# Where a layer-norm tile is transposed: by DMA or on TensorE, in the last forward pair of a four-layer attention kernel

## The chip, the cores and the metric

The kernel runs on one core of a Trainium2 chip, as one launch. The metric is the device time of that launch in microseconds. Before the change the median of seven runs is 2477.54 us (2466.08 to 2485.54).

## What is computed

Four residual layers run over a sequence of 2048 rows of width 640, with 32 heads of 20 columns. Layers 0 and 2 are of kind A (linear attention), layers 1 and 3 of kind B (softmax attention in a causal window of 256 rows). Both A layers share their weights, as do both B layers. The kernel returns the output and the gradients of the input and of the four weights.

```python
x = A_x
x = x + _A_ref(_layernorm(x), A_wqkv, A_wo)
x = x + _B_ref(_layernorm(x), B_wqkv, B_wo)
x = x + _A_ref(_layernorm(x), A_wqkv, A_wo)
x = x + _B_ref(_layernorm(x), B_wqkv, B_wo)
# _A_ref: phi(q) @ (sum over rows of phi(k)^T v), divided by phi(q) . sum phi(k); then @ wo
# _B_ref: softmax(q k^T * 20**-0.5 inside the window) @ v; then @ wo
# returned: x, and the vjp of x for grad_out with respect to A_x and the weights
```

## The kernel before

The rows lie in 16 tiles of 128. The forward pass has a first segment (the first half of layer 0) and two calls of `seg_pair`: the first finishes layer 0, runs layer 1 and begins layer 2; the second, which the text calls the last pair, finishes layer 2, runs layer 3 and already begins the backward pass (it computes dO, the gradient at the attention's output). The backward pass follows, in stages of its own, and reads what the forward pass stored.

`seg_pair` interleaves two streams. One is the attention itself: for each tile b and each of 8 groups g of four heads it makes scores (L410), exponentials on ScalarE (L416), masks on GpSimd (L419, L422) and products with the values (L438). The other is `step(b)`, a Python generator that walks through a list called `plan`: pairs of a function and an offset, so that `(qkv, 1)` in step b works on tile b + 1. Each function yields how many matmul columns it has issued; the loop takes pieces from the generator until the amount `work`, spread over the 8 groups, is reached. In the last pair the functions are: `mix`, the read-out of layer 2 and its transposed tile oT; `proj1`, the output projection of layer 2 and the layer norm before layer 3; `qkv`, the q, k and v of layer 3; `fetch_g`, which loads and transposes grad_out; `proj2`, the output projection of layer 3; and `do`, which computes dO. The first three steps (b = -3 to -1) run ahead of the attention; after that `steady[0]` is true.

The layer norm is `ln`. It makes statistics on VectorE (L217, L219), the reciprocal deviation on ScalarE (L221, L223) and the normalised rows ln_hn on VectorE (L225). The matmuls of qkv (L358) need these rows transposed, as ln_hnT. In steady tiles `pt()` is None, and a DMA on SyncE's queue does that (`tr`, L152). Otherwise `flip` does it: five TensorE transposes against the identity (L715) into a PSUM tile and one copy out (L717). SyncE also stores the plain rows for the backward pass (L125, hn).

`B_qkv` ends with three DMA transposes of its q, k and v slabs into the ring tiles (L152), from which the scores read, and with stores of the ring to DRAM (`keep`, the tensor qkvT) on ScalarE's DMA queue, half a pair of tiles in each call.

A tile scheduler turns this traced order into one order for each engine, by readiness and priority, and hands out the tiles of a pool as they come free. Four PSUM banks (pool `psd`, the tiles named d) serve all projections, transposes and value products; two tiles (`pss`, the tiles named s) hold scores. Each engine then works through its own order strictly, and each DMA queue too.

Of the kernel before, what the change touches and what calls it, by code (L numbers as in the profile page):

```python
# [16 lines left out]
P = 128  # L17
# [6 lines left out]
class Kern:  # L24

    def __init__(self, ctx, tc, x0, A_wqkv, A_wo, B_wqkv, B_wo, grad_out, outs):
# [4 lines left out]
        self.H = H = D // DH  # L31
        self.G = H // 4
        self.TT = TT = T // P
# [74 lines left out]
        for l in (1, 3):  # L108
            self.sv[l] = dict(
                qk=d.tile([P, TT, 2 * D], BF, name=f"qk{l}"),  # L110
                qkvT=d.tile([P, 3 * self.G, T], BF, name=f"qkvT{l}"),
                dOT=d.tile([P, self.G, T], BF, name=f"dOT{l}"),
                dO=d.tile([P, TT, D], BF, name=f"dO{l}"))
# [95 lines left out]

    def ln(self, l, tt, pw, pt=None):
        nc, D = self.nc, self.D
        x = self.car[:, tt, :]
        st = pw.tile([P, 2, nc.vector.BN_STATS_DIM], F32, name="ln_st")
        for c in range(2):
            nc.vector.bn_stats(st[:, c, :], x[:, c * self.HD:(c + 1) * self.HD])  # L217
        mv = pw.tile([P, nc.vector.BN_AGGR_DIM], F32, name="ln_mv")
        nc.vector.bn_aggr(mv, st)  # L219
        lv = pw.tile([P, 1], F32, name="ln_lv")  # L220
        nc.scalar.activation(lv, mv[:, 1:2], ACT.Ln, bias=self.eps_t, scale=1.0)  # L221
        rs = self.rs[l][:, tt:tt + 1]
        nc.scalar.activation(rs, lv, ACT.Exp, scale=-0.5)  # L223
        hn = pw.tile([P, D], BF, name="ln_hn")
        nc.vector.tensor_scalar(out=hn, in0=x, scalar1=mv[:, 0:1], scalar2=rs, op0=ALU.subtract, op1=ALU.mult)  # L225
        hnT = pw.tile([P, self.DT, P], BF, name="ln_hnT")
        if pt is None:
            self.tr(hnT, hn)
        else:
            self.flip(hn, self.DT, hnT, pt, [nc.scalar.copy])  # L230
        self.dma(self.hn_d[l][:, tt, :], hn, nc.sync)
        return hnT

    def flip_o(self, l, tt, o, pw, pt=None):
        oT = pw.tile([P, self.DT, P], BF, name="oT")
# [113 lines left out]

    def B_qkv(self, l, tt, hnT, W, qk, v, ring, pps):  # L350

        nc = self.nc
        qkv = qk.rearrange("p (h d) -> p h d", d=HP)
        vv = v.rearrange("p (h d) -> p h d", d=HP)
        for ci in range(4):
            ps = pps.tile([P, 512], F32, name="d")[:, 0:480]
            for k in range(self.DT):
                nc.tensor.matmul(ps, lhsT=hnT[:, k, :], rhs=W[:, k, ci * 480:(ci + 1) * 480],  # L358
                                 start=(k == 0), stop=(k == self.DT - 1))
            h0, h1 = ci * 24, (ci + 1) * 24  # L360
            for t, base, n in ((qkv, 0, 2 * self.H), (vv, 2 * self.H, self.H)):
                a, b = max(h0, base), min(h1, base + n)
                if a < b:
                    dst, src = t[:, a - base:b - base, 0:DH], self.hv(ps)[:, a - h0:b - h0]
                    if ci % 2 == 0:
                        nc.vector.tensor_copy(dst, src)
                    else:
                        nc.scalar.copy(dst, src)  # L368
            yield self.DT * 480
        G = self.G  # L370
        for i, src in enumerate((qk[:, 0:G * P], qk[:, G * P:], v)):
            self.tr(self.ring_at(ring, i, tt), src)
        for i in range(2):
            flat = self.pw_fwd.tile([P, self.D], BF, name="qk_flat")
            nc.vector.tensor_copy(self.hv(flat), qkv[:, i * self.H:(i + 1) * self.H, 0:DH])
            self.store(self.sv[l]["qk"][:, tt, i * self.D:(i + 1) * self.D], flat)

        def keep(pair, i, g0, g1):
            src = self.ring_at(ring, i, 2 * pair, 2)
            return (self.sv[l]["qkvT"][:, i * G + g0:i * G + g1, 2 * pair * P:(2 * pair + 2) * P], src[:, g0:g1, :])  # L380
        parts = (((0, 0, G), (1, 0, G // 2)), ((1, G // 2, G), (2, 0, G)))
        if tt >= 2:
            for x in parts[tt % 2]:
                self.dma(*keep(tt // 2 - 1, *x))
        if tt == self.TT - 1:
            self.ring_tail = [keep(tt // 2, *x) for x in parts[0] + parts[1]]

# [99 lines left out]
    def seg_pair(self, l, acc, on_tail=None):  # L487

        nc, TT, H, G = self.nc, self.TT, self.H, self.G
        with ExitStack() as st:  # L490
            pW = self.pool(st, "fw")
            pw = self.pool(st, "fww", 2)
# [5 lines left out]
            last = l + 2 > 3  # L498
            if last:
                self.B_do_setup(pW, 2, 2)  # L500
            oT1, hn1, oT2, hn2 = {}, {}, {}, {}
            self.close_A(acc)
            mbd = self.mbd
            if not last:
# [12 lines left out]
            ring = [pW.tile([P, G, n * P], BF, name=f"ring{i}") for i, n in enumerate((4, 6, 4))]  # L517
            self.score_blocks, spreads = [], []
            tiles = []
            steady = [False]  # L520
# [10 lines left out]
            bank = Bank()  # L531

            def pt():
                return None if steady[0] else banks
# [6 lines left out]

            def proj1(t):
                yield from self.out_proj(t, oT1.pop(t), WoA, pps)
                hn1[t] = self.ln(l + 1, t, pw, pt())

            def qkv(t):
                yield from self.B_qkv(l + 1, t, hn1.pop(t), WB, qks[t % 2], slabs[t % len(slabs)], ring, pps)
# [30 lines left out]


            if last:  # L580
                plan = ((mix, 3), (qkv, 1), (proj1, 2), (fetch_g, -1), (proj2, -1), (do, -1))
                work, skip = 21300, (9600, 4600)
            else:
                plan = ((mix, 3), (qkv, 1), (proj1, 2), (first_half, -2), (proj2, -1))
                work, skip = 27000, (5000, 0)
# [931 lines left out]
```

## Time and profile before

| what | value |
|---|---|
| median of 7 runs | 2477.54 us (2466.08 to 2485.54) |
| the profiled execution's own time | 2485.54 us |
| its span, first to last instruction | 2483.8 us |
| granted TensorE clock, mean | 0.925 |
| busy: TensorE, VectorE, ScalarE, GpSimd | 88%, 62%, 49%, 40% |
| in 560:860 us, the steady tiles of the last pair | 84%, 71%, 59%, 58% |
| granted TensorE clock in 560:860 us | 0.94 |

A wait in the profile reads "who waited, for whom: total us, how often, the longest". A line of the timeline reads "start us, length us, engine, line, operation, written tile<-read tiles, shape, how many in a row [idle time before, and what ended it]". A line of windows gives the stretch and its length, then the busy time (and the number of instructions) of TensorE, its weight loads, VectorE, ScalarE and GpSimd, then the granted clock, the busy share of the DMA engines and GB/s.

### The profile page before, as it was taken

How to read it: one execution, taken by the hardware profiler on the slowest of the kernel's cores; microseconds unless marked ns; L12 is line 12 of the kernel's file. 1: busy time of each engine (PE TensorE's matmuls, PEld its weight loads, DVE VectorE, ACT ScalarE, POOL GpSimd, SP SyncE). 2: the span in 40 equal slices, each digit the busy share in tenths (PEclk: the TensorE clock that was granted, in tenths of full speed). 3: DMA queues.
4: the chain of work that ended last, by engine and by line, in shares of the span. 5: the costliest groups of instructions: out<-in, count | busy, mean ns of one | idle time of the engine just before them, and what ended most of it. 6: DMA issues, size and time to landing. Idle time of an engine off the chain costs nothing.

```text
span 2483.8 us, 68598 instructions
## 1 busy us (share of the span) xinstructions
PE 2179.1 (88%) x27602; PEld 1501.3 (60%) x27602; DVE 1544.2 (62%) x3022; ACT 1224.6 (49%) x1957; POOL 986.0 (40%) x1528
## 2 busy tenths in 40 slices
PE   6879989878788879999989799689999979979999
PEld 4635555544445536777657577467777756656455
DVE  6657767557766747778756577456676656646212
ACT  4447767635555646777733344455665543333000
POOL 4436656545555624444433333233343333311000
PEclk9989999978989957999989999689999979989999
DMA  8599888477888798797989596899988979588787
GB/s 248 149 186 202 185 176 179 130 175 171 199 181 183 178 260 160 151 158 139 189 187 235 131 242 192 217 219 197 189 178 168 192 175 232 151 228 231 191 268 217
DMA packets 895233, 474.37 MB, mean 191 GB/s; under 512 B 626752, under 2 KB 873280, under 8 KB 894912
## 3 DMA queue, kind: packets, MB, share of 16 engines
q1 hardware_dynamic: 782288, 338.72, 65.1%
q0 software_dynamic: 24768, 84.57, 10.4%
q10 hardware_dynamic: 87856, 46.68, 6.8%
q8 instruction: 216, 3.54, 0.6%
q14 instruction: 105, 0.86, 0.1%
HBM read 187.07 MB, written 161.19 MB: 140 GB/s over the span
## 4 chain that ended last, share of the span: by engine, by line
PE 36%; DMA 7%; issue 6%; DVE 5%; SPq 3%; POOL 2%; ACT 2%; ACTq 0%; DVEq 0%; POOLq 0%
PE acc L950 8%; PE acc L1024 7%; PE wg L1363 6%; PE sp L890 5%; PE d L758 5%; PE tp L934 3%; POOL do_o L738 2%; SPq L125 2%; PE t L715 1%; DVE ds L924 1%; ACT e L904 1%; DVE car L775 1%; DMA dsT<-ds 1%; DMA wg_r<-dqkv 1%; SPq L152 1%
## 5 line engine op out<-in xcount | busy, mean ns | idle before, releaser
L924 DVE SCALAR_TENSOR_TENSOR ds<-sp,e 128x768 bf16<-128x768 f32 (+2 forms) x512 | 462.9, 906 | 255.9 <-PE sp L890 159.6
L904 ACT ACTIVATE e<-sp 128x768 bf16<-128x768 f32 (+2 forms) x512 | 394.4, 777 | 238.4 <-PE sp L890 170.2
L416 ACT ACTIVATE e<-s 128x1024 bf16<-128x1024 f32 x360 | 359.9, 1025 | 139.8 <-PE s L410 113.6
L908 POOL TENSOR_SCALAR_AFFINE_SELECT e<-e 128x512 bf16<-128x512 bf16 x256 | 163.0, 637 | 422.9 <-ACT e L904 414.9
L410 PE MATMUL s<-qbd,ring 128*128 128x512 bf16 x720 | 247.9, 393 | 16.1 <-ACT e L416 12.2
L358 PE MATMUL d<-W,ln_hnT 128*128 128x480 bf16 x640 | 173.0, 405 | 42.2 <-DMA ln_hnT<-ln_hn 36.0
L1024 PEld LDWEIGHTS <-wg_l 128*128 128x128 bf16 x2800 | 191.4, 101 | 30.4 <-issue 13.3
L890 PE MATMUL sp<-VT,dOT 32*128 32x384 bf16 (+2 forms) x1024 | 181.3, 341 | 27.0 <-ACT e L904 23.1
L419 POOL TENSOR_SCALAR_AFFINE_SELECT e<-e 128x512 bf16<-128x512 bf16 x256 | 165.1, 646 | 96.2 <-ACT e L416 94.5
L890 PE MATMUL sp<-KT,QT 32*128 32x384 bf16 (+2 forms) x1024 | 185.3, 346 | 13.1 <-ACT e L904 6.0
L1363 PE MATMUL wg<-wg_r,wg_l 128*128 128x480 bf16 (+1 forms) x960 | 177.4, 348 | 5.3 <-DMA wg_r<-dqkv 2.8
L265 PE MATMUL d<-W,ln_hnT 128*128 128x320 bf16 x960 | 155.8, 312 | 29.4 <-ACT v_slab L368 11.9
L422 POOL TENSOR_SCALAR_AFFINE_SELECT e<-e 128x512 bf16<-128x512 bf16 x224 | 146.0, 652 | 85.9 <-ACT e L416 84.5
L1024 PE MATMUL acc<-wg_r,wg_l 128*128 128x160 bf16 x1840 | 157.6, 240 | 12.7 <-DMA wg_r<-dqkv 6.2
L758 PE MATMUL d<-WT,dqkvT 128*128 128x320 bf16 x960 | 145.5, 306 | 10.7 <-DMA dqkvT<-dqkv 10.7
L1363 PEld LDWEIGHTS <-wg_l 128*128 128x128 bf16 x960 | 95.0, 99 | 87.5 <-issue 7.9
L265 PEld LDWEIGHTS <-ln_hnT 128*128 128x128 bf16 x960 | 96.0, 101 | 83.1 <-issue 27.6
L438 PEld LDWEIGHTS <-e 128*128 128x128 bf16 x2880 | 113.0, 97 | 53.9 <-POOL e L419 9.7
L912 POOL TENSOR_SCALAR_AFFINE_SELECT e<-e 128x512 bf16<-128x512 bf16 x224 | 142.3, 635 | 0.0
L934 PE MATMUL tp<-ident,ds 128*128 128x128 bf16 x1440 | 136.0, 234 | 6.0 <-DVE ds L924 2.7
L358 PEld LDWEIGHTS <-ln_hnT 128*128 128x128 bf16 x640 | 65.8, 106 | 118.7 <-DMA ln_hnT<-ln_hn 43.7
L950 PEld LDWEIGHTS <-dsT 128*128 128x128 bf16 x2880 | 93.9, 98 | 68.2 <-issue 47.9
(192 smaller groups left out, 4395.7 us busy)
## 6 DMA issues: line engine op xcount, KB each, us to landing
qkvT<-ring ACTq DMA_DIRECT2D x32, 512.0 KB, 4.3
dqkv<-dqkv_o POOLq DMA_DIRECT2D x64, 240.0 KB, 4.1
wg_r<-dqkv SPq DMA_DIRECT2D x64, 240.0 KB, 4.4
hn<-ln_hn SPq DMA_DIRECT2D x64, 160.0 KB, 2.4
qk<-qk_flat POOLq DMA_DIRECT2D x64, 160.0 KB, 4.2
qk_r<-qk SPq DMA_DIRECT2D x32, 320.0 KB, 4.3
hn_ld<-hn SPq DMA_DIRECT2D x64, 160.0 KB, 3.2
dqkv<-dkv_t POOLq DMA_DIRECT2D x32, 320.0 KB, 4.4
```

Of the source, the lines that this page charges most:

```text
L265: nc.tensor.matmul(ps, lhsT=hnT[:, k, :], rhs=W[:, k, ci * HD:(ci + 1) * HD], start=(k == 0), stop=(k == self.DT - 1))
L358: nc.tensor.matmul(ps, lhsT=hnT[:, k, :], rhs=W[:, k, ci * 480:(ci + 1) * 480], start=(k == 0), stop=(k == self.DT - 1))
L410: nc.tensor.matmul(ps[:, i, :], lhsT=self.ring_at(ring, 1, kt)[:, g, :], rhs=self.qbd[b % 2][:, g, :, :], start=True, stop=True)
L416: nc.scalar.activation(e[:, 0:i + 1], ps[:, 0:i + 1], ACT.Exp, scale=self.c_att)
L758: self.nc.tensor.matmul(ps[:, c, 0:self.HD], lhsT=w, rhs=WT[:, k, c * self.HD:(c + 1) * self.HD], start=(k == 0), stop=(k == len(lhs) - 1))
L890: nc.tensor.matmul(ps[:, j, 0:nkt * P], lhsT=slabs[g][ta][r0:r0 + HP, b * P:(b + 1) * P], rhs=slabs[g][tb][r0:r0 + HP, k0 * P:(k0 + nkt) * P],
L904: nc.scalar.activation(ev[:, 2 * half:2 * half + 2], ps[:, :, 0:nkt * P].rearrange("p h (i k) -> p h i k", k=P), ACT.Exp, scale=c_att)
L924: nc.vector.scalar_tensor_tensor(out=dv[:, hs], in0=ps[:, :, 0:nkt * P].rearrange("p h (i k) -> p h i k", k=P), scalar=c_att, in1=ev[:, hs ...
L934: nc.tensor.transpose(tp[:, i * P:(i + 1) * P], ds_of[u][:, (nb + i) * P:(nb + i + 1) * P], self.ident)
L950: x.append(nc.tensor.matmul(acc[:, hh * DH:hh * DH + w], lhsT=lhsT, rhs=rhs(rname, g, t, hh, w), start=(i == 0), stop=(i == len(s) - 1), s ...
L1024: x = self.nc.tensor.matmul(ps[:, 0:w], lhsT=lhs(t), rhs=rhs(t), start=(t == 0), stop=(t == self.TT - 1), skip_group_check=True)
L1363: nc.tensor.matmul(ps, lhsT=lhs[:, tt, rows], rhs=rhs[:, tt, 0:w], start=(tt == 0), stop=(tt == TT - 1))
```

## The change

Three things change. `ln` can leave out the transposition (`later`) and return the rows and the empty tile; in steady tiles of the last pair a new function `flip_hn` then transposes them on TensorE, between `proj2` and `do` of the same step. The plan of the last pair is put in another order, with qkv and proj1 ahead of mix, and with slightly larger amounts in `work` and `skip`. In `B_qkv`, for both pairs, the stores of the ring are traced at the head of the function, before the matmuls and the new transposes. Line numbers after the diff are 2 to 13 higher.

```diff
@@ ln
-    def ln(self, l, tt, pw, pt=None):
+    def ln(self, l, tt, pw, pt=None, later=False):
...
-        if pt is None:
+        if later:
+            pass
+        elif pt is None:
             self.tr(hnT, hn)
         else:
             self.flip(hn, self.DT, hnT, pt, [nc.scalar.copy])
         self.dma(self.hn_d[l][:, tt, :], hn, nc.sync)
-        return hnT
+        return (hn, hnT) if later else hnT
@@ B_qkv
+        def keep(pair, i, g0, g1):
...
+        parts = (((0, 0, G), (1, 0, G // 2)), ((1, G // 2, G), (2, 0, G)))
+        if tt >= 2:
+            for x in parts[tt % 2]:
+                self.dma(*keep(tt // 2 - 1, *x))
         qkv = qk.rearrange("p (h d) -> p h d", d=HP)
...
-        def keep(pair, i, g0, g1):
...
-        if tt >= 2:
-            for x in parts[tt % 2]:
-                self.dma(*keep(tt // 2 - 1, *x))
@@ seg_pair
             def proj1(t):
                 yield from self.out_proj(t, oT1.pop(t), WoA, pps)
-                hn1[t] = self.ln(l + 1, t, pw, pt())
+                late = last and steady[0]
+                hn1[t] = self.ln(l + 1, t, pw, pt(), late)
+                if late:
+                    unflipped.append(t)
+
+            def flip_hn(t):
+                for x in unflipped:
+                    hn, hnT = hn1[x]
+                    self.flip(hn, self.DT, hnT, bank, [nc.scalar.copy])
+                    hn1[x] = hnT
+                unflipped.clear()
+                yield 640
...
             if last:
-                plan = ((mix, 3), (qkv, 1), (proj1, 2), (fetch_g, -1), (proj2, -1), (do, -1))
-                work, skip = 21300, (9600, 4600)
+                plan = ((qkv, 1), (proj1, 2), (mix, 3), (fetch_g, -1), (proj2, -1), (flip_hn, 2), (do, -1))
+                work, skip = 21900, (9600, 5200)
```

More of the change, by code (lines that the diff above doesn't have):

```diff
@@ L350, in B_qkv @@
     def B_qkv(self, l, tt, hnT, W, qk, v, ring, pps):
-        nc = self.nc
+        nc, G = self.nc, self.G
+        def keep(pair, i, g0, g1):
+            src = self.ring_at(ring, i, 2 * pair, 2)
+            return (self.sv[l]["qkvT"][:, i * G + g0:i * G + g1, 2 * pair * P:(2 * pair + 2) * P], src[:, g0:g1, :])
+        parts = (((0, 0, G), (1, 0, G // 2)), ((1, G // 2, G), (2, 0, G)))
+        if tt >= 2:
+            for x in parts[tt % 2]:
+                self.dma(*keep(tt // 2 - 1, *x))
         qkv = qk.rearrange("p (h d) -> p h d", d=HP)
@@ L369, in B_qkv @@
             yield self.DT * 480
-        G = self.G
         for i, src in enumerate((qk[:, 0:G * P], qk[:, G * P:], v)):
@@ L376, in B_qkv @@
             self.store(self.sv[l]["qk"][:, tt, i * self.D:(i + 1) * self.D], flat)
-        def keep(pair, i, g0, g1):
-            src = self.ring_at(ring, i, 2 * pair, 2)
-            return (self.sv[l]["qkvT"][:, i * G + g0:i * G + g1, 2 * pair * P:(2 * pair + 2) * P], src[:, g0:g1, :])
-        parts = (((0, 0, G), (1, 0, G // 2)), ((1, G // 2, G), (2, 0, G)))
-        if tt >= 2:
-            for x in parts[tt % 2]:
-                self.dma(*keep(tt // 2 - 1, *x))
         if tt == self.TT - 1:
@@ L500, in seg_pair @@
                 self.B_do_setup(pW, 2, 2)
-            oT1, hn1, oT2, hn2 = {}, {}, {}, {}
+            oT1, hn1, oT2, hn2, unflipped = {}, {}, {}, {}, []
             self.close_A(acc)
```

## The prediction

> **What bounds the kernel now.** I read the page's forty slices first (TensorE is at 6 to 9 tenths everywhere, so a microsecond that it idles inside a stage is a microsecond of the span), then asked which stretch the edited code fills. Its own lines, the qkv matmuls L358 with layer-norm tiles that a DMA transposed, run from 548 to 846 us in the last forward pair. So I took the waits of TensorE and the sums of 560:860, 13 tiles of about 22.7 us (first L358 of successive tiles at 659.80, 683.75, 706.03, 730.66).
>
> ```profile
> PE d L358 <- DMA ln_hnT<-ln_hn: 31.4, 11, 4.6
> PE d L249 <- ACT v_slab L368: 5.1, 4, 1.8
> PE d L715 <- DVE oT L717: 4.5, 4, 3.0
> PE d L358 <- DVE do_slab L749: 4.0, 1, 4.0
> ...
> 560.00:860.00 300.00, 251.02 (x2632) 150.61 (x2632) 212.00 (x464) 176.32 (x216) 173.50 (x285) 0.94 0.82 183
> ```
>
> The second line kind sums the stretch: TensorE 251 of 300 us, VectorE 212, ScalarE 176, GpSimd 174, granted clock 0.94, DMA share 0.82. TensorE idles 49.0 us; 31.4 of it waits for the transposed layer-norm rows, and the 4.0 put down to do_slab is the same wait (matmul at 730.66, transpose issued at 727.42, as in the other tiles). That is 35.4 us. TensorE is the fullest engine, but VectorE follows at 71%.
>
> One tile in the timeline, TensorE, then the queue of SyncE, VectorE and GpSimd:
>
> ```profile
> 683.75 2.18 PE L358 MATMUL d<-W,ln_hnT 128*128 128x480 bf16 x5 [4.54 <-DMA ln_hnT<-ln_hn]
> ...
> 692.12 1.17 PE L358 MATMUL d<-W,ln_hnT 128*128 128x480 bf16 x5
> ...
> 697.19 0.44 PE L715 MATMUL d<-ident,g_ld 128*128 128x128 bf16 x5
> 697.47 0.38 PE L410 MATMUL s<-qbd,ring 128*128 128x512 bf16 x1
> ```
> ```profile
> 679.98 1.87 SPq L152 DMA_TRANSPOSE ln_hnT<-ln_hn  x1
> ```
> ```profile
> 677.22 2.73 DVE L225 TENSOR_SCALAR ln_hn<-car,ln_mv,rs 128x640 bf16<-128x640 bf16 x1
> ...
> 701.74 1.06 DVE L225 TENSOR_SCALAR ln_hn<-car,ln_mv,rs 128x640 bf16<-128x640 bf16 x1
> ```
> ```profile
> 678.55 0.63 POOL L419 TENSOR_SCALAR_AFFINE_SELECT e<-e 128x512 bf16<-128x512 bf16 x1
> 679.14 0.63 POOL L422 TENSOR_SCALAR_AFFINE_SELECT e<-e 128x512 bf16<-128x512 bf16 x1
> ```
>
> Three things are to be seen. The normalised rows are ready at 679.95, the transpose is issued at once, and the matmul starts 3.8 us later: latency, with nothing ahead of it in the queue. Two: the first five matmuls after the wait take 2.18 us, the fifth lot 1.17, so the wait also costs clock (the windows 684:688 and 688:692 have 0.50 and 0.82). Three: the rows are late in every second tile, since L225 takes 2.73 us there and ends as a run of GpSimd selects ends; it takes 1.06 in the others. The waits alternate likewise: 2.1, 4.5, 2.1, 4.0, 2.1.
>
> **What the Trainium skill says.** "TensorE: Matmul & The Clock Gate", "What's actually happening": the array drops to half clock after an idle window of about 3.4 us and needs a busy one to come back. The trace agrees: a mean of 0.94 over 300 us is 36 us at half. "VectorE: DVE Perf Modes", "The three transpose paths": 390 ns for a 128x128 bf16 block on TensorE, 1309 ns by DMA. Here five blocks on TensorE take 0.28 us of its queue (697.19 to 697.47; one alone lasts 218 ns), and a DMA of five lands 3.2 us after issue (median); the trace decides. "GPSIMD Engine Reference", specifications table: GpSimd's path to SBUF is shared with VectorE where that runs in its two-port mode; the 2.73 us agrees with that, as L225 is the SBUF-to-SBUF kind.
>
> **The change part by part.** The order of instructions in the two built programs shows what moves. Up to the last pair nothing moves on any engine, so the first pair, which calls the edited B_qkv too, stays as it is. In the last pair's steady tiles:
>
> 1. Fourteen DMA transposes of ln_hn leave SyncE's queue (1.2 us of it each). The waits for them go: 35.4 us of TensorE. The qkv that uses a tile now comes a tile's end later than its flip. With it goes the slow clock: 36 us at half, all but 3.4 us of it right behind these waits; at some 80% busy, half of 33 us is 13 us. Sum gained: 48.
>
> 2. Added on TensorE: 14 x 5 transposes, 0.28 us per five: 4 us. Added on ScalarE: 14 copies at 0.69 us (the row of this copy from another PSUM tile), 10 us. ScalarE is busy 59%, and the copy has two dO groups, two value groups and four score matmuls (1.36 + 0.6 + 0.85 = 2.8 us) before the next L358. Hidden; without that cover 10 us.
>
> 3. The plan's order is now qkv, proj1, mix, ..., proj2, flip, do. The flip stands on TensorE directly behind ten proj2 matmuls, so what waits behind it is everything: dO, scores, values, next qkv. Is ln_hn there in time? Between the last proj1 matmul and the flip TensorE has 7 scores (0.21 each, 1.47), mix (0.44), ten transposes (0.56), two value groups (0.60) and proj2 (two lots of 0.68): 4.43 us. VectorE over the same time has, in its new order, the second residual add 0.42, two qbd copies 0.88, bn_stats 0.42, mix's two rinv steps 0.39, bn_aggr 0.12, flip_t 0.42, o_t 0.89, gT 0.40, ln_hn 0.98 (701.74 to 702.72): 4.9, with the start about 5.0. So TensorE waits about 0.55 us in a plain tile, and 2.2 us if ln_hn takes 2.65. Behind ln_hn stand a qbd copy and a residual add (0.87) whose PSUM bank the first dO group takes, against 0.49 of TensorE's work: 0.4 more. New waits: 1.0 in a plain tile, 2.6 in a long one; with 7 plain and 6 long, 22.6 us. Bounds: 0 (VectorE ahead throughout) to 4.5 per tile (below).
>
> 4. mix moves behind qkv and proj1. Its output is transposed by DMA for proj1 of the next tile, about 13 us ahead of use; 4.9 us is the median landing of the larger ring transposes. Hidden. What it delays: proj2's banks come from o_t, 0.2 us; it sits inside the chain of step 3. The 4.5 + 0.8 us that g_ld's flip and L249 now wait for oT and gT mostly go, because oT is copied before proj1's add: 4 us gained; bounds 0 and 5.3.
>
> 5. The row stores qkvT<-ring are traced before the transposes, but on ScalarE they still stand between the two copies of qkv in the odd tiles and wait for the same transpose of that tile. The 10.2 us that ScalarE waits so, and TensorE's 5.1 us, I leave at no change; bounds -5 and +6 (the dO transposes go just ahead of them on SyncE). This wait also bunches the exponentials, and so the selects that lengthen ln_hn; hence I keep the long tiles.
>
> 6. The hn row store follows later in SyncE's queue and nothing waits for it. work 21300 to 21900 spreads the added 640 over the same eight groups; skip moves the end of the pair by under a group: nothing, bounds one wait either way (2 us).
>
> Sum: -48 + 4 - 4 + 22.6 = -25. The profiled execution, 2485.5 us with a span of 2483.8, would be about 2460. It is the slowest of the seven runs shown, 8 us over their median; from 2477.5, 2452 us.
>
> **Rivals.** All: TensorE never waits for ln_hn, VectorE having 29% free; ln_hn takes 1.06 everywhere. For it: VectorE idled 3.1 and 2.8 us in the tile of 683 in waits for qkv's and proj1's matmuls. Against: from the mix on its queue is unbroken. Then -48 + 4 - 4 = -48: 2430 us.
>
> The wait only changes its place: ln_hn ended 6.7 us (702.8 against 696.1) and 9.0 us (679.95 against 670.95) after proj1's last matmul. With the cover of 4.4 us TensorE would stand 2.3 and 4.6 us at the flip, and lose clock again: 44 + 13 + 4 against 48 + 4 gained, 9 us more: 2486 us. For it: the in-order queue. Against: those times held two proj2 adds, an o_b and a dO_t ahead of ln_hn, which the new order puts behind.
>
> Slower: every tile becomes a long one, at the flip. With no pauses of TensorE the selects come closer, ln_hn needs 2.7 us each time, rs arrives behind an exponential of 1.02, and what is behind the flip starts cold. That is 4.5 us x 13 = 58, clock 13, transposes 4, less 52: +23, 2500 us. It decides where the mean wait at the flip and dO passes 2.7 us with the clock still lost (52 - 13 - 4 = 35 over 13 tiles), and shows as slower by 0.5% from 3.6 us.
>
> That the change doesn't do what it says is true of the row stores alone (step 5).
>
> **How the numbers follow.** A measurement of this kernel can tell about 0.5%, 12 us, from no change. Forecast 0.52, own range 2440 to 2463; all 0.22 (2425 to 2440); wait in a new place, in whole or half, 0.16 (2464 to 2490); slower 0.10 (over 2490). Leaving out the slow case and the outer parts of its neighbours gives 2426 to 2474. Faster: 0.52 + 0.22 + a little of the third case, 0.77; same 0.13; slower 0.10.
>
> **What would show it.** Right: no wait of L358 for a DMA in the last pair; ln_hn transposes on TensorE, 70 more, waiting for VectorE's L225 for 0.5 to 2.5 us each; clock of the stretch 0.97 or more; a tile of 20 to 21 us; ScalarE's v_slab still waiting for the ring's DMA. Wrong: waits over 3 us at the flip, or L358 waiting for ScalarE's copy of ln_hnT, or a tile under 19.5 us, or stages outside the last pair that move by more than a few us.

## The result, and the profile after

The changed kernel takes 2460.42 us (median of 14 runs, 2448.8 to 2469.33), the kernel before 2476.14 us in the runs beside it: a ratio of 0.9931, with a 95% interval of 0.9912 to 0.9949. That is 13 to 22 us less. The prediction of 2452 us had the direction right and expected 25 us; about two thirds of it came.

The profiled execution has a span of 2457.9 us. The first matmul of the backward pass after the last pair (the sp group) starts at 863.4 us in place of 882.5, so 19.1 of the 25.9 us between the two profiles lie before the end of the last pair, 18.0 of them inside it. The rest is in stages whose instructions did not change. Such stages vary by a few us from one execution to the next: in the traces of versions that leave the first pair alone it ends between 494.1 and 503.7 us.

The waits of TensorE in the last pair of the changed kernel (500:870 us), the longest in total first: who waited for whom, us in total, times, longest.

```profile
PE s L412 <- ACT e L418: 28.2, 13, 3.7
PE s L728 <- DVE ln_hn L225: 4.6, 2, 2.5
PE d L728 <- DVE ln_hn L225: 4.1, 1, 4.1
...
PE d L728 <- DVE flip_t L201: 3.5, 8, 0.7
...
PE d L811 <- DVE car L253: 2.9, 7, 0.5
```

The wait for the transposed layer-norm rows, 33.1 + 4.0 us over that window before, is gone, as was said. The flip waits for ln_hn for 4.1 us once, in the first steady tile, and hardly again (the 4.6 us are the first steps, which were there before with 5.3). A new line stands at the head: the scores L412 wait 28.2 us for ScalarE to have emptied a score tile. Before, in the same window:

```profile
PE s L410 <- ACT e L416: 1.0, 3, 0.6
```

What ScalarE waits for, in 540:840 us of the same kernel:

```profile
ACT v_slab L378 <- DMA ring<-qk_slab: 23.1, 6, 4.9
ACT e L418 <- DMA dOT_ring<-do_slab: 17.6, 4, 5.4
...
ACT e L418 <- DMA ring<-qk_slab: 4.3, 1, 4.3
```

The last of these stands right behind a store of dOT (issued at 587.29 us), like the four above it. Before, the first was 10.2 us and the second did not occur (540:840 us):

```profile
ACT v_slab L368 <- DMA ring<-qk_slab: 10.2, 4, 3.2
...
ACT e L416 <- DMA ring<-qk_slab: 2.1, 1, 2.1
```

The timeline of ScalarE and its DMA queue in two successive tiles, then TensorE in the same two:

```profile
655.66 0.37 ACTq L125 DMA_DIRECT2D qkvT<-ring  x1
656.07 0.56 ACT L378 CAST v_slab<-d 128x480 bf16<-128x480 f32 x1 [3.78 <-DMA ring<-qk_slab]
...
675.38 0.57 ACTq L125 DMA_DIRECT2D dOT<-dOT_ring  x1
676.05 1.02 ACT L418 ACTIVATE e<-s 128x1024 bf16<-128x1024 f32 x1 [4.05 <-DMA dOT_ring<-do_slab]
```
```profile
657.61 0.59 PE L412 MATMUL s<-qbd,ring 128*128 128x512 bf16 x2 [2.58 <-ACT e L418]
...
677.13 0.83 PE L412 MATMUL s<-qbd,ring 128*128 128x512 bf16 x2 [2.07 <-ACT e L418]
```

A store is issued from ScalarE's own sequence of instructions. It waits for a transpose that SyncE has only just issued, ScalarE idles 3.8 and 4.05 us at it, and the exponentials behind it come late. In the odd tiles it is the store of the ring, in the even ones the store of dOT. TensorE, with two score tiles, stands 1.5 to 3.7 us in nearly every tile: 15.9 us in the tiles with the ring's store, 12.0 in those with dOT's.

The tiles became shorter by less than hoped: the first qkv matmuls of tiles 592.2 to 818.8 before are 22.7 us apart (ten tiles), those from 579.3 to 819.5 after are 21.8 (eleven). The third of the late tiles already begins 12.9 us earlier (579.3 for 592.2); the tiles after it and the end of the pair add 6.2.

### The profile page after: what moved, and what is told of

The parts are those of the page before. It is cut to its first block, busy times and chain, and to the rows that moved or that the text cites. A ratio compares the mean times of both kernels' runs of the same rounds, so it can differ in the third digit from the quotient of the medians.

```text
span 2457.9 us, 68721 instructions
## 1 busy us (share of the span) xinstructions
PE 2171.7 (88%) x27672; PEld 1504.4 (61%) x27672; DVE 1534.9 (62%) x3022; ACT 1236.8 (50%) x1971; POOL 988.9 (40%) x1528
## 4 chain that ended last, share of the span: by engine, by line
PE 37%; DMA 7%; issue 6%; DVE 5%; SPq 4%; POOL 2%; ACT 2%; ACTq 0%; DVEq 0%; POOLq 0%
PE acc L963 7%; PE acc L1037 7%; PE wg L1376 6%; PE sp L903 5%; PE d L771 5%; PE tp L947 3%; POOL do_o L751 2%; SPq L125 2%; PE t L728 2%; DVE ds L937 1%; DVE car L788 1%; ACT e L917 1%; SPq L152 1%; DMA wg_l<-o 1%; DMA pk_ld<-pk 1%
## 5 line engine op out<-in xcount | busy, mean ns | idle before, releaser
L412 PE MATMUL s<-qbd,ring 128*128 128x512 bf16 x720 | 247.6, 397 | 41.8 <-ACT e L418 38.9
L903 PE MATMUL sp<-VT,dOT 32*128 32x384 bf16 (+2 forms) x1024 | 181.5, 342 | 27.0 <-ACT e L917 22.7
L267 PE MATMUL d<-W,ln_hnT 128*128 128x320 bf16 x960 | 154.3, 310 | 28.1 <-ACT v_slab L378 10.8
L1037 PE MATMUL acc<-wg_r,wg_l 128*128 128x160 bf16 x1840 | 159.0, 242 | 11.7 <-DMA wg_l<-o 5.0
L368 PE MATMUL d<-W,ln_hnT 128*128 128x480 bf16 x640 | 156.8, 376 | 5.6 <-DMA ln_hnT<-ln_hn 3.7
L267 PEld LDWEIGHTS <-ln_hnT 128*128 128x128 bf16 x960 | 95.4, 101 | 80.7 <-issue 27.5
L963 PE MATMUL acc<-qk_r,dsT 128*128 128x40 bf16 (+1 forms) x2880 | 118.9, 181 | 13.7 <-DMA dsT<-ds 12.0
```

Of the source, the lines that this page charges most:

```text
L267: nc.tensor.matmul(ps, lhsT=hnT[:, k, :], rhs=W[:, k, ci * HD:(ci + 1) * HD], start=(k == 0), stop=(k == self.DT - 1))
L412: nc.tensor.matmul(ps[:, i, :], lhsT=self.ring_at(ring, 1, kt)[:, g, :], rhs=self.qbd[b % 2][:, g, :, :], start=True, stop=True)
L903: nc.tensor.matmul(ps[:, j, 0:nkt * P], lhsT=slabs[g][ta][r0:r0 + HP, b * P:(b + 1) * P], rhs=slabs[g][tb][r0:r0 + HP, k0 * P:(k0 + nkt) * P],
L963: x.append(nc.tensor.matmul(acc[:, hh * DH:hh * DH + w], lhsT=lhsT, rhs=rhs(rname, g, t, hh, w), start=(i == 0), stop=(i == len(s) - 1), s ...
L1037: x = self.nc.tensor.matmul(ps[:, 0:w], lhsT=lhs(t), rhs=rhs(t), start=(t == 0), stop=(t == self.TT - 1), skip_group_check=True)
```

## The experiments

Three theories. A: the flip on TensorE gained the time. B: the new order of the plan gained it, since it alone gives the DMA transpose the end of the tile to land in. C: what kept the rest away is ScalarE standing at the stores. Ratios are to the kernel before, measured beside each run.

The third part of the change has no run of its own. In the first pair it acts alone, and up to the end of that pair the traces before and after the change show the same instructions in the same order on all five engines (one store's issue apart, which runs beside an instruction that starts at the same time). There the scheduler put these stores where it had put them before. That it does so in the last pair too was not tried by itself.

### The order alone

```diff
-                late = last and steady[0]
+                late = False
-                plan = (..., (proj2, -1), (flip_hn, 2), (do, -1))
-                work, skip = 21900, (9600, 5200)
+                plan = (..., (proj2, -1), (do, -1))
+                work, skip = 21300, (9600, 4600)
```

> The new order of the plan alone: the layer-norm rows are still transposed by DMA, work and skip as before the change. If the order is what gained (the transpose then has the rest of the tile to land), L358's counterpart waits under 10 us for the DMA and the ratio to the kernel before is 0.991 to 0.996. If the flip on TensorE is what gained, the DMA wait stays over 25 us in the stretch and the ratio is 0.998 to 1.002.

Measured: 0.996 (0.9942 to 0.9978), at the upper bound of what B expected, and by its waits of the other kind:

```profile
PE d L368 <- DMA ln_hnT<-ln_hn: 30.6, 8, 5.5
```

The order alone gains some 10 us, but the matmuls still wait for the DMA, more rarely and longer. Neither theory is cleared by this run. A part of the waits can be read off SyncE's queue, in two successive tiles, with the matmuls that follow:

```profile
639.11 1.75 SPq L152 DMA_TRANSPOSE ln_hnT<-ln_hn  x1
...
658.11 1.71 SPq L152 DMA_TRANSPOSE oT<-o_t  x1
659.87 0.58 SPq L125 DMA_DIRECT2D o<-o_t  x1
660.54 1.20 SPq L152 DMA_TRANSPOSE ln_hnT<-ln_hn  x1
```
```profile
643.48 1.19 PE L368 MATMUL d<-W,ln_hnT 128*128 128x480 bf16 x5
...
666.12 1.19 PE L368 MATMUL d<-W,ln_hnT 128*128 128x480 bf16 x5 [3.61 <-DMA ln_hnT<-ln_hn]
```

In every second tile the transpose of oT and the store of o stand ahead of that of ln_hn. It is issued 1.7 us after its rows are ready at 658.83 (1.7 to 3.0 us in the six such tiles from 577 us on), its matmuls start 3.9 to 7.3 us after that, and these are the tiles in which TensorE waits. In the tiles between them it is issued within 0.25 us, and TensorE does not wait.

### The flip alone, in the old order

```diff
-                plan = ((qkv, 1), (proj1, 2), (mix, 3), (fetch_g, -1), ...)
+                plan = ((mix, 3), (qkv, 1), (proj1, 2), (fetch_g, -1), ...)
```

> The flip on TensorE late in the tile, with the old order (mix, qkv, proj1). If the flip is what gained, the ratio is 0.990 to 0.996. If the order is what gained, proj1 ends too late in the tile, TensorE waits for ln_hn at the flip (over 15 us in all), and the ratio is 0.997 to 1.003.

Measured: 0.9945 (0.9924 to 0.9967), A's range; the interval also touches B's. TensorE waits for ln_hn at the flip: the wait that the prediction feared, in this order and not in that of the change.

```profile
PE d L728 <- DVE ln_hn L225: 14.2, 13, 4.9
```

So the parts alone give some 10 and 14 us, both together 17 (medians beside the same kernel before: ratios 0.996, 0.9945, 0.9931). They do not add, as two ways round one wait would not. Each half alone gives more than half of the gain; these runs do not make one of them its cause.

### The stores kept back

`keep_in_program_order` puts an instruction behind everything traced before it on its engine. With it the stores are issued half a tile to a tile later, when their transposes have landed.

```diff
             for x in parts[tt % 2]:
-                self.dma(*keep(tt // 2 - 1, *x))
+                d = self.dma(*keep(tt // 2 - 1, *x))
+                if l == 3:
+                    self.tc.keep_in_program_order(d)
...
-            self.do_late()
+            self.tc.keep_in_program_order(self.do_late())
```

> The changed kernel, with the stores of the ring and of dOT kept behind everything traced before them on ScalarE, about a tile later than now, when their transposes have landed. Theory: ScalarE's standing at these stores (23 + 18 us) is what holds TensorE's scores for 28 us; then these waits vanish and the kernel is 18 to 28 us faster than the changed one, ratio to before 0.981 to 0.987. Rival: ScalarE or VectorE set the pace and the stores only show their slack; then the waits move elsewhere and the ratio stays at 0.990 to 0.995.

Measured: 2426.96 us, 0.9811 (0.977 to 0.9852). C holds: no wait of ScalarE for a DMA is left in 540:840 us, none of L412's counterpart for ScalarE among TensorE's longest, and the tiles from 580.0 to 789.0 are 19.0 us apart. The sums of these eleven tiles, in the columns explained with the profile before:

```profile
580.00:789.00 209.00, 193.28 (x2176) 122.46 (x2210) 168.88 (x382) 152.92 (x187) 144.26 (x231) 1.00 0.94 211
```

TensorE is busy 92% at full clock, VectorE 81%. The gain over the changed kernel is 33 us between the two medians, which were not taken side by side. Taken through the ratios to the kernel before it is 30 us, and 19 us in the repeat below. The traces agree with TensorE's wait of 28.2 us as the main part of it; a part should be the clock that this wait had pulled down (0.96 in 560:840 us of the changed kernel), less what TensorE now waits for VectorE (8.0 us for flip_t and 6.0 for car at dO, where it was 3.5 and 2.9).

The same edit on the kernel before, where the stores are traced at the end of B_qkv:

> The kernel before, with the same stores kept back in the same way. Theory: its waits for the ring at ScalarE hide largely behind the wait for ln_hnT, only 5 us of TensorE hang on them, and long ln_hn tiles may go with them: ratio 0.994 to 0.999. Rival: the stores were as dear before as after: ratio 0.985 to 0.991.

Measured: 1.003 (1.0012 to 1.0048). The theory had said slightly faster; it is slightly slower. The waits for the ring are gone, and TensorE waits elsewhere (before the change, with the stores kept back, 500:870 us):

```profile
PE d L358 <- DMA ln_hnT<-ln_hn: 22.5, 11, 3.6
PE d L335 <- DVE dO_t L801: 13.8, 10, 1.8
```

So in the kernel before these stores cost nothing: other waits filled the same time. They became dear only once the change had taken the cover away. The run also shows that I had the cause of the long L225 wrong. The rows that normalise ln_hn, of this kernel and of the changed one with the stores kept back (minimum/median/maximum ns, 540:840 us):

```profile
L225 DVE TENSOR_SCALAR ln_hn<-car,ln_mv,rs x13: 583/2550/3129, 554.3 to 827.6; 128x640 bf16<-128x640 bf16 x13
```
```profile
L225 DVE TENSOR_SCALAR ln_hn<-car,ln_mv,rs x14: 437/666/1135, 539.6 to 784.7; 128x640 bf16<-128x640 bf16 x14
```

I had put the length down to exponentials bunched by ScalarE's wait. Without the wait it is longer. In the runs with the new order, or with the flip, it is short (0.43 to 1.13 us, once 1.97). What its length goes with is how many of GpSimd's selects run beside it. In the 13 traces, 540:840 us, it took 0.43 to 0.44 us with none (19 cases), 0.43 to 0.79 with one (122), 0.62 to 1.97 with two (13) and 2.09 to 3.13 with three or four (18). In all of the last 18 it ends 0.19 us after the last select of an unbroken run. The Trainium skill ("SBUF — State Buffer", "SBUF: two separate sides") says that VectorE in a two-port mode and GpSimd hold a shared pair of ports one instruction at a time, each blocking the other. The spread from 0.43 to 3.13 us for one form agrees with that, though here it lasted through up to four selects and not one. Ending so evenly behind the run is what waiting for it would look like; moving the selects by themselves was not tried.

### Which store

> The changed kernel with only the stores of the ring kept back; the dOT stores wait as they did. ScalarE stood 23 + 4 us at the first kind and 18 us at the second. If the two costs add, this takes 55 to 65% of what keeping both back took (33 us between the two medians): 18 to 22 us less than the changed kernel, ratio to before 0.984 to 0.988. If a tile pair is paced by the worse of the two, it takes under a third of it: 0.989 to 0.993.

> The changed kernel with only the dOT stores kept back; the stores of the ring wait as they did. If the two costs add: 10 to 15 us less than the changed kernel, ratio 0.987 to 0.990; if not, 0.990 to 0.994.

Measured: the ring's stores kept back alone 0.984 (0.9809 to 0.9871), the dOT stores alone 0.9891 (0.9863 to 0.9918). Medians 21 and 11 us below the changed kernel's, both within what adding costs would give. But whether they add is not settled. 21 and 11 fit the 33 us of the first run with both kept back; the repeat below, at 0.9853, is no faster against its kernel before than the ring's stores alone. And the expectation's split, 27 and 18 us of ScalarE's waiting, counted the 4.3 us behind a dOT store with the ring: by place it is 23.1 and 21.9. With only the ring's stores kept back, ScalarE's waits at the dOT stores nearly go as well (540:840 us):

```profile
ACT v_slab L380 <- DMA dOT_ring<-do_slab: 2.3, 2, 1.2
```

With only dOT kept back TensorE still waits 21.2 us for ScalarE. So the ring's store is the dearer one.

### Which half of the change is needed

> The new order of the plan with both stores kept back, and the rows still transposed by DMA. If the flip on TensorE is needed, L358's counterpart still waits over 20 us for the DMA and the ratio is 0.990 to 0.997, as the order alone gave. If the order was enough and only the stores stood in its way, it comes to within 0.3% of the version with both parts (0.981).

> The flip on TensorE and both stores kept back, in the old order (mix, qkv, proj1). If the new order is needed beside the flip, TensorE waits for ln_hn at the flip for over 15 us and the ratio is 0.985 to 0.993. If not, it is within 0.3% of 0.981.

The edits are those of the two halves above, each with both stores kept back. Measured: the order with DMA transposes 2428.68 us, 0.9805 (0.9778 to 0.9831); the flip in the old order 2457.92 us, 0.9928 (0.9899 to 0.9957). With the stores kept back the order is enough, and the flip in the old order is not. The order's wait for the DMA, in 500:870 us:

```profile
PE d L730 <- DVE flip_t L201: 6.3, 11, 0.6
PE d L370 <- DMA ln_hnT<-ln_hn: 6.2, 6, 1.6
```

From 30.6 to 6.2 us, with the transpose on the same queue. But its place in that queue is another:

```profile
649.93 1.20 SPq L152 DMA_TRANSPOSE ln_hnT<-ln_hn  x1
...
651.85 1.65 SPq L152 DMA_TRANSPOSE oT<-o_t  x1
```

In every tile from 573 us on it now stands ahead of oT's, and is issued within 0.35 us of its rows. So the edit did more than hold the stores back: the scheduler also put SyncE's queue in another order. How much of the gain from 0.996 to 0.9805 is due to either was not separated; in the run of the order alone ScalarE waits only 7.1 us for DMAs in 540:840 us. In the old order the flip waits for ln_hn (12.7 us, under the 15 expected), the scores for qbd (13.8) and the transposes for oT (11.7); with the stores not kept back it was 14.2, 9.0 and 8.3.

Both good versions once more, beside each other:

> The same kernel as the changed one with both stores kept back, beside the next run on one chip: ratio to before 0.978 to 0.984. If the flip on TensorE is worth anything with this order and these stores, it is more than 0.3% (7 us) below the next run.

> The same kernel as the new order with both stores kept back and the rows transposed by DMA: 0.978 to 0.984. If the flip is worth nothing here, it is within 0.3% of the run before it, on either side.

Measured: with the flip 2433.94 us, 0.9853 (0.9826 to 0.988); with DMA transposes 2427.7 us, 0.9832 (0.9808 to 0.9856). The first missed its expected range of 0.978 to 0.984. On top of the new order, with the stores kept back, the flip gains nothing that can be measured; if anything it costs a little. There B holds and A falls. Without the stores kept back each half gains by itself.

The traces allow one more reading, free of what the other stages do: the time from the last qkv matmul of the first pair (L265, later L267) to the first of the sp group, one execution each. By it the flip alone gains as much as the whole change, and on top of the order, with the stores kept back, it costs 3 to 10 us.

| version | last pair, us |
|---|---|
| before; with both stores kept back | 383.9; 384.4 |
| order alone; flip alone; the change | 369.8; 365.4; 365.9 |
| the change, ring's stores kept back; dOT's; both (two runs) | 342.5; 355.1; 339.3 and 338.9 |
| order alone, both stores kept back (two runs) | 329.7 and 336.2 |
| flip in the old order, both kept back | 359.7 |

### A faster version

The first pair uses B_qkv too, and there ScalarE stands at the ring's stores as well. Without the condition on the layer:

```diff
-                if l == 3:
-                    self.tc.keep_in_program_order(d)
+                self.tc.keep_in_program_order(d)
```

> Both stores kept back, and the stores of the ring in the first pair too, where ScalarE stands 30 us at them and TensorE's L267 and L412 wait 22 us for ScalarE. If the wait is as dear there, 8 to 20 us below the version that keeps back only the last pair's: ratio 0.972 to 0.978. If VectorE or the projections hold that pair anyway: 0.979 to 0.984.

Measured: 2407.04 us (2401.68 to 2410.78), 0.9742 (0.9717 to 0.9767), 27 us below the version that keeps back only the last pair's, beside it. This is more than the 8 to 20 us expected; the ratio is in the expected range. In its trace the first pair ends at 478.0 us. The waits of TensorE in 90:500 us, the first pair, of the changed kernel and of this one:

```profile
PE d L267 <- ACT v_slab L378: 10.8, 4, 3.5
PE s L412 <- ACT e L418: 10.8, 12, 2.4
```
```profile
PE s L729 <- DVE ln_hn L225: 7.6, 3, 3.2
PE d L267 <- DVE pk_t L283: 6.1, 10, 1.9
```

The two waits for ScalarE are no longer among the longest. This version, the change with these two edits, beats both kernels.

## Why the prediction was right or wrong

**The bound and the wait that goes (step 1): right.** The 35 us are gone, and so is part of the slow clock: in 540:840 us TensorE ran at half clock for 47.8 us before and for 24.7 us after. I had counted on nearly all of it; the new waits take the clock down again, at 677 us for instance. I had also cited an idle window of about 3.4 us as what takes the clock down, and said that the trace agrees. It agrees in part: before the change, waits of 2.12 us (at 614.57) and 2.11 (at 706.03) were followed by half clock too, and one of 2.14 (at 659.80) was not. The first two late tiles gave more than I had for them, 12.9 us by the start of the third. That qkv no longer stands behind mix in the first steady step is a likely reason, not one tried.

**What is added (step 2): right.** There are 70 more matmuls, and the copies on ScalarE stay hidden; in the steady tiles nothing waits for them.

**The flip (step 3): too dear.** The term was 22.6 us. In its place the runs show about 0.4 us at the flip in all steady tiles but the first (4.1 us there, which the sum of 13 tiles left out), and 2.9 us at dO. VectorE's side of the race was right: ln_hn is ready 4.5 to 5.4 us after proj1's last matmul in these tiles, where I had 4.9. TensorE's side was too short: it comes to the flip after 4.8 to 6.4 us, where I had 4.43. And the six long tiles did not exist, because L225 takes 0.43 to 0.76 us in the new order. The reason I gave for them, in step 5, fell with the kernel before whose stores were kept back.

**Mix (step 4): half of the gain.** The waits for oT and gT go from 5.8 us to 0.2 in the tiles, but the transposes of g_ld now wait 3.5 us for flip_t: some 2 us gained in place of 4.

**The stores on ScalarE (step 5): this is the step that failed.** I saw that tracing them earlier moved nothing and that ScalarE would still stand there, and set the change at none, between -5 and +6 us. Measured: ScalarE waits 45 us at these stores where it waited 12, and TensorE hangs on ScalarE for 28.2 us where it hung for 6.1 (5.1 at L249, 1.0 at the scores). I priced the wait by what it cost beside the longer one that the change removes, and asked only whether its instruction moved, not whether what hid it stayed. The dOT store did not enter the sum at all. The dO transpose that it waits for is issued 3.6 us into the tile (671.14, the tile at 667.5) where it was issued 0.9 us into it (684.61, the tile at 683.75); the store follows 4.2 us later.

**The sum.** The two errors, at the stores some 22 us too little and at the flip some 19 us too much, nearly cancelled, and that was luck; with the clock that came back only in part, 17 us were left of 25. Of the signs named for being right, two came: no wait of L358's counterpart for a DMA, and v_slab still waiting for the ring. The clock of the stretch (0.96), the tile (21.8 us) and the waits at the flip did not. The rival that had TensorE never wait for ln_hn describes the flip well, but its 2430 us come only once the stores are kept back (2427 to 2434). Then TensorE works 17.6 us, at full clock, in a tile of 19.0. The rival of the wait that moves to the flip is right in kind for the old order alone, at 1.1 us per tile and not 2.3 to 4.6. Slower did not come near.

**Open.** How much of what keeping the stores back gains with the order alone is ScalarE's, and how much is the other place of the transpose in SyncE's queue. Whether the costs of the two stores add. And that GpSimd's selects set the length of L225, which was not tried by itself.

## What to carry to other kernels

When a change removes the longest wait of a stage, list every other wait on the queues of that stage at its full length on its own engine, not at what it costs today beside the one removed. Here 12 us of ScalarE's waiting, of which 6 reached TensorE, became 45, of which 28 did. A DMA issue that waits, on an engine that also computes, is an instruction like any other; look for it where that engine idles "for a DMA", and put it where its input has landed. And test each half of a change by itself, also with the new bound taken away: with the stores kept back, the order was worth some 2%, the move to TensorE 1% by itself and nothing on top of the order. Look then at what else such an edit has moved.

## What the hardware showed that I had not expected

One form of a VectorE instruction, the 128x640 bf16 normalisation from SBUF to SBUF, took 0.43 to 3.13 us, longer the more of GpSimd's selects ran beside it; the 18 longest cases all ended 0.19 us after a run of three or four selects. A gap of TensorE of 2.07 us, at 677 us, was followed by 3.4 us of half clock, while one of 2.58 us at 657.6 us was not.
